# Three 512-token and two 384-token groups in place of six of 384, the first group's first products in halves, attention in pairs of blocks, and weights converted in place

## The chip, the core and the metric

The kernel runs on one core of a Trainium2 chip. The metric is the device time of one execution in microseconds (us). In the traces PE is the matrix engine (PEld its weight loads), DVE the vector engine, ACT the scalar engine, POOL the GpSimd engine, and SP the engine whose queue issues every DMA here.

## What is computed

Three stages follow one another. Attention looks back over a window of 64 positions, the second stage is a two-layer network with a Mish activation, and the third is one with a softmax-weighted activation (SoLU) and a layer norm. All of it is to be exact to fp32.

```python
batch, n_heads, seq, head_dim = (4, 8, 576, 64)          # 2304 tokens, d_model 512
scores = scale * q @ k.T;  mask = (rel >= 0) & (rel < 64)
attn = softmax(where(mask, scores, -1e9));  x = attn @ v  # [2304, 512]
h = x @ w_in                                              # 512 -> 2048
x = (h * tanh(softplus(h))) @ w_out                       # Mish, 2048 -> 512
h = x @ w_in2                                             # 512 -> 1024
solu = h * softmax(h)
out = layernorm(solu) * g_ln @ w_out2                     # 1024 -> 512
```

## The kernel before

**Products.** Each fp32 operand of the network stages is split into a part of 12 bits (hi) and the rest (lo), and a product is three matmuls: hi by hi, hi by lo, lo by hi. The weights come as 64-bit floats: 32 bits in `st[:, :, 1]` (upper) and 32 in `st[:, :, 0]` (lower), side by side, so that each half is read with a stride of two words. A *piece* is 128x512 weights; w_in (called w1) and w_out (w2) have 16 pieces each, w_in2 (w3) and w_out2 (w4) 8 each. One piece costs a load into `st` and six steps: `c_up` (L322) scales the upper half into a tile `wf`, `c_low` (L332) the lower half into `wl`, `c_bits` (L338) and `c_sign` (L344) put the fp32 weight together in `wf`, `c_hi` (L359) rounds it to hi, and `c_lo` (L364) takes lo. `st` and `wf` have 3 buffers each, `wl` has 2. The first 4 pieces lie in a room of their own, `room_b`.

**Attention.** The 2304 tokens are 36 blocks of 64. For one block, `a_qk` writes the scores of 8 heads into one PSUM bank (128x512), and DVE scales and masks them (`a_scale`, L469), takes the maximum (`a_max`, L475) and subtracts it (`a_sub`, L481). ACT takes the exponential (`a_exp`, L489) and DVE the sum (`a_sum`, L493) and its reciprocal (`a_norm`). POOL multiplies (`a_mul`, L504), PE transposes (`a_tr`), ACT copies (`a_pt`), and PE multiplies by the values (`a_pv`). ACT and DVE then write hi and lo of x (`a_x`, `a_xl`). Scores, transposes and results share the pool `ps_a`, two buffers of one bank. The first 6 blocks, which are the first group, go by another way (`a_max0`, L451; `a_exp0`, L459): the mask is added by a matmul, and the exponential takes the maximum as its bias and gives the sum itself, one call for each pair of heads.

**Mish stage.** The tokens are six groups of 384. One *iteration* (j, f) takes group j and 128 hidden units f. `pe_m1` (L574) makes 12 matmuls of 384 columns into `ps_h`, ACT applies Mish (L597), hi and lo of the result are taken (`g_h`, L263 or L267; `g_l`, L283), and `pe_m2` and `pe_m2l` add 8 and 4 matmuls to four accumulators x_0 to x_3 (one bank each). Groups 0 and 1 are done for f 0 to 7 and then for f 8 to 15, so that the weights of the second half are needed later. Their first halves are stored (`part_d`) and added at the end. Attention of group j+1 runs beside the products of group j.

**Third stage.** 18 tiles of 128 tokens: 24 matmuls (L715), the SoLU and the norm on DVE, ACT and POOL, 8 transposes (L763) and 24 matmuls (L788).

**Order.** `Schedule` is a list scheduler that runs while the program is built. Each step has a cost on one or more engines, a due time (from the number of its iteration and tables such as `MISH_AT`, `ATT_AT`, `CONV_PRIO`) and the buffers that it needs, and the scheduler gives out the order of the instructions of each engine. At run time each engine takes its own list strictly in order and waits on semaphores. ACT reloads its function table (ACT_TABLE_LOAD) between an exponential and a Mish.

Of the kernel before, what the change touches and what calls it, by code (L numbers as in the profile page):

```python
# [14 lines left out]
F32 = mybir.dt.float32  # L15
# [9 lines left out]
P = 128  # L25
BLK = 64
LD = 2
CUT = 8
# [6 lines left out]
    "up0": {"act": 0.57, "pool": 0.846}, "up": {"act": 0.57},  # L35
    "pt0": {"act": 0.5}, "x0": {"act": 0.29}, "pt": {"act": 0.5}, "x": {"act": 0.29},
    "w0_hi": {"dve": 0.36, "act": 0.51}, "w0_lo": {"dve": 0.63, "pool": 1.5},
    "w_hi": {"act": 0.51, "dve": 0.36}, "w_lo": {"dve": 0.63, "pool": 1.5},
    "w4_hi": {"act": 0.613}, "w4_lo": {"dve": 0.663},
    "g_hi": {"dve": 0.28, "act": 0.42}, "g_lo": {"dve": 0.48},  # L40
    "x2": {"act": 0.39, "dve": 0.5},
# [15 lines left out]
G_AT = 10.0
K0_LATER = -3.349
W_STEP = 5.115
M4_LATER = -0.753  # L60
# [118 lines left out]
def attention_moe_solu(  # L179
# [27 lines left out]
    GROUPS = [384] * 6  # L207
# [3 lines left out]
    N0 = GROUPS[0] // BLK  # L211
    assert N0 <= NBB
    GMAX = max(GROUPS)
# [35 lines left out]
    st_p = actx.enter_context(tc.tile_pool(name="st", bufs=3))  # L249
# [8 lines left out]
    ps_a = tctx.enter_context(tc.tile_pool(name="ps_a", bufs=2, space=PSUM, side="right"))  # L258
# [62 lines left out]

    def c_up(e, p):  # L322
        p["wf"] = st_p.tile([P, 512], F32, tag="wf", name="wf")
        w = p["st"][:, :, 1].bitcast(F32)
        if e == "act":
            nc.scalar.activation(out=p["wf"], in_=w, func=ACTF.Copy, scale=2.0**-112)  # L326
        else:
            nc.gpsimd.tensor_scalar(
                out=p["wf"], in0=w, scalar1=2.0**-112, scalar2=0.0, op0=ALU.mult, op1=ALU.add
            )  # L330

    def c_low(p):  # L332
# [49 lines left out]
    NI = NF * NG  # L382
    needs += [NI - NF + 4 + W_STEP * (n + 1) for n in range(2 * KD + NF2)]
# [21 lines left out]
    def open_q0():  # L405
        room["q"] = wpool.tile([P, N0 + 1, NP, P], F32, tag="w1", name="room_q")
# [27 lines left out]
    def a_qk(n):  # L434
        ps = ps_a.tile([P, NP, P], F32, tag="a", name="ps_s")
        r = room["r"]
        for p in range(NP):
            early = n < N0
            nc.tensor.matmul(out=ps[:, p, :], lhsT=qt[n][:, p, :], rhs=kt[n][:, p, :], start=True, stop=not early)  # L439
            if early:  # L440

                nc.tensor.matmul(
# [642 lines left out]
```

## Time and profile before

| | |
|---|---|
| time, median of 3 runs | 740.83 us (740.2 to 741.36) |
| the profiled execution's own time | 740.77 us |
| its span, first to last instruction | 739.0 us |
| granted PE clock, mean | 0.988 |
| busy: PE, DVE, ACT, POOL | 706.6, 425.4, 295.8, 156.3 us |

The span leaves 1.77 us of the time outside. Busy time of PE is an upper bound on its work, because neighbouring matmuls overlap in the records: a matmul of 384 columns has a record of 341 ns, and the next one starts after 173 ns. What a stage costs PE is therefore read from how far apart the starts of two stages lie where PE never waits. Busy shares are means over stages with different limits, so the stages are to be read one by one.

### The profile page before, as it was taken

The numbers are of one execution on the slowest core, as the hardware profiler recorded it, in microseconds if no ns is written. First come the engines' busy times: TensorE is split into PE (matmuls) and PEld (weight loads), VectorE is DVE, ScalarE is ACT, GpSimd is POOL, SyncE is SP. The second block draws the span as 40 slices with busy tenths as digits, with TensorE's granted clock in tenths as the row PEclk, the third lists the DMA queues.
The fourth block names the chain that finished last, engine by engine and source line by source line (L and its number), as shares of the span: only waits on it lengthen the run. The fifth ranks groups of instructions, "written<-read, shape, count | busy, mean of one in ns | idle before, by whom it ended". The sixth has DMA issues, their size and how long they took to land.

```text
span 739.0 us, 11115 instructions
## 1 busy us (share of the span) xinstructions
PE 706.6 (96%) x4344; PEld 653.2 (88%) x4344; DVE 425.4 (58%) x734; ACT 295.8 (40%) x551; POOL 156.3 (21%) x176
## 2 busy tenths in 40 slices
PE   6797889699999999999999999999999999999998
PEld 5696789699999999999999999999888888888886
DVE  3999999955645334424434412676575646464642
ACT  4665435454454345334434433345432323232221
POOL 3556644421111011011101110331122111121000
PEclk9899999899999999999999999999999999999999
DMA  8645565652622201302222011331111111111001
GB/s 299 243 155 196 163 213 173 192 178 98 192 83 100 86 30 58 129 29 75 69 88 70 1 44 58 114 114 58 59 43 57 43 43 43 43 44 43 29 16 43
DMA packets 42916, 70.45 MB, mean 95 GB/s; under 512 B 3312, under 2 KB 27376, under 8 KB 42864
## 3 DMA queue, kind: packets, MB, share of 16 engines
q1 hardware_dynamic: 42864, 69.75, 28.6%
q8 instruction: 34, 0.56, 0.3%
q14 instruction: 18, 0.15, 0.1%
HBM read 58.72 MB, written 11.01 MB: 94 GB/s over the span
## 4 chain that ended last, share of the span: by engine, by line
PE 85%; DVE 10%; issue 2%; ACT 1%; DMA 1%; POOL 0%; SPq 0%; DVEq 0%; ACTq 0%; POOLq 0%
PE ps_h L587 24%; PE x L621 16%; PE h L715 14%; PE po L788 13%; PE x L632 8%; PE ps_s L439 4%; DVE wf L346 3%; DVE wf L340 3%; PE pt L763 2%; PE ps_o L541 2%; PE ps_t L518 2%; DVE g L283 1%; DVE w L267 1%; DMA room_q<-qk 0%; DVE su L493 0%
## 5 line engine op out<-in xcount | busy, mean ns | idle before, releaser
L587 PE MATMUL ps_h<-xt,w 128*128 128x384 f32 x1152 | 221.5, 341 | 5.6 <-POOL w L281 2.0
L587 PEld LDWEIGHTS ps_h<-xt,w 128*128 128x128 f32 x1152 | 204.5, 191 | 8.3 <-POOL w L281 2.8
L621 PE MATMUL x<-g,w 128*128 128x384 f32 x768 | 153.5, 340 | 9.4 <-ACT xs L657 6.2
L621 PEld LDWEIGHTS x<-g,w 128*128 128x128 f32 x768 | 134.9, 190 | 12.0 <-ACT xs L657 6.9
L283 DVE SCALAR_TENSOR_TENSOR g<-mc,g 128x384 fp32r<-128x384 f32 x96 | 69.8, 728 | 109.2 <-ACT g L263 108.5
L597 ACT ACTIVATE mc<-ps_h 128x384 f32<-128x384 f32 x96 | 47.0, 490 | 154.9 <-PE ps_h L587 154.6
L715 PE MATMUL h<-w,xs 128*128 128x512 f32 x432 | 104.2, 396 | 0.4 <-DVE y L734 0.4
L788 PE MATMUL po<-w,lz 128*128 128x512 f32 x432 | 102.3, 393 | 0.0
L715 PEld LDWEIGHTS h<-w,xs 128*128 128x128 f32 x432 | 80.8, 188 | 19.6 <-PE x L632 0.7
L504 POOL TENSOR_TENSOR s<-s,rs 128x512 f32<-128x512 f32 x36 | 40.6, 1145 | 257.3 <-DVE rs L498 109.7
L788 PEld LDWEIGHTS po<-w,lz 128*128 128x128 f32 x432 | 80.0, 188 | 16.4
L632 PE MATMUL x<-g,w 128*128 128x384 f32 x384 | 84.1, 340 | 0.0
L632 PEld LDWEIGHTS x<-g,w 128*128 128x128 f32 x384 | 67.6, 189 | 0.7
L334 POOL TENSOR_SCALAR wl<-st 128x512 uint32<-128x512 uint32 x44 | 37.6, 855 | 63.5 <-DMA st<-w_in 20.1
L722 DVE TENSOR_REDUCE nm<-h 128x1 f32<-128x1024 f32 x18 | 22.0, 1224 | 49.1 <-PE h L715 49.1
L263 ACT ACTIVATE g<-mc 128x384 fp32r<-128x384 f32 x87 | 45.8, 526 | 4.9 <-PE x L632 2.2
L326 ACT ACTIVATE wf<-st 128x512 f32<-128x512 f32 x44 | 29.3, 672 | 45.3 <-DMA st<-w_in 21.0
L706 POOL TENSOR_TENSOR xs<-xr,xs 128x512 fp32r<-128x512 f32 x18 | 23.3, 1294 | 95.2 <-ACT xs L701 95.2
L281 POOL TENSOR_TENSOR w<-wf,w 128x512 fp32r<-128x512 f32 x22 | 33.1, 1510 | 43.9 <-DVE w L267 40.3
L346 DVE SCALAR_TENSOR_TENSOR wf<-st,wf 128x512 uint32<-128x512 uint32 x44 | 40.5, 921 | 1.2
L340 DVE SCALAR_TENSOR_TENSOR wf<-wf,wl 128x512 uint32<-128x512 uint32 x48 | 40.8, 851 | 0.1
L701 ACT ACTIVATE xs<-xr 128x512 fp32r<-128x512 f32 x18 | 11.4, 632 | 62.9 <-PE h L715 46.9
(75 smaller groups left out, 671.9 us busy)
## 6 DMA issues: line engine op xcount, KB each, us to landing
qk<-qk SPq DMA_DIRECT2D x30, 512.0 KB, 4.4
st<-w_out SPq DMA_DIRECT2D x24, 512.0 KB, 3.6
st<-w_in SPq DMA_DIRECT2D x20, 512.0 KB, 3.8
v<-v SPq DMA_DIRECT2D x30, 256.0 KB, 2.8
x2d<-xs SPq DMA_DIRECT2D x24, 192.0 KB, 2.1
xr<-x2d SPq DMA_DIRECT2D x18, 256.0 KB, 3.1
out<-o SPq DMA_DIRECT2D x18, 256.0 KB, 2.0
room_b<-w_in SPq DMA_DIRECT2D x4, 512.0 KB, 7.8
```

The costliest lines, as they stand in the source:

```text
L263: nc.scalar.activation(out=hi, in_=x, func=ACTF.Copy, scale=1.0 if g is None else g)
L283: nc.vector.scalar_tensor_tensor(out=lo, in0=x, scalar=1.0 if g is None else g, in1=hi.bitcast(F32), op0=ALU.mult, op1=ALU.subtract)
L334: nc.gpsimd.tensor_scalar(out=p["wl"], in0=p["st"][:, :, 0], scalar1=0.9325 * 2.0**-29, scalar2=0.0, op0=ALU.mult, op1=ALU.add)
L340: nc.vector.scalar_tensor_tensor(out=wb, in0=wb, scalar=3, in1=p["wl"], op0=ALU.logical_shift_left, op1=ALU.bitwise_or)
L346: nc.vector.scalar_tensor_tensor(out=wb, in0=p["st"][:, :, 1], scalar=0x80000000, in1=wb, op0=ALU.bitwise_and, op1=ALU.bitwise_or)
L504: nc.gpsimd.tensor_tensor(out=s, in0=s, in1=rs.to_broadcast([P, NP, P]), op=ALU.mult)
L587: nc.tensor.matmul(out=ps[:, :n], lhsT=w[:, a, k, fs], rhs=x[:, b, k, :n], start=(idx == 0), stop=(idx == len(terms) - 1),)
L597: nc.scalar.activation(out=c[:, :n], in_=ht.pop(i)[:, :n], func=ACTF.Mish)
L621: nc.tensor.matmul(out=acc[j][m][:, :n], lhsT=w[:, a, f % 4, m * P:(m + 1) * P], rhs=g[:, 0, :n], start=(i in opens and a == 0), stop=False,)
L632: nc.tensor.matmul(out=acc[j][m][:, :n], lhsT=w[:, 0, f % 4, m * P:(m + 1) * P], rhs=g[:, 1, :n], start=False, stop=i in closes,)
L715: nc.tensor.matmul(out=h2[t][:, c, :], lhsT=x[:, a, k, :], rhs=wt["w3", c][:, b, k, :], start=(idx == 0), stop=(idx == len(terms) - 1),)
L788: nc.tensor.matmul(out=po[t], lhsT=lz[:, a, f, :], rhs=wt["w4", f // 4][:, b, f % 4, :], start=(c == 0 and idx == 0), stop=(c == 2 and idx ...
```

## The change

- `GROUPS` becomes 512, 512, 512, 384, 384. The first four f of group 0 are done in two halves of 256 columns (`HALF`), so `its` has 84 iterations: 8 of 256 columns, 44 of 512 and 32 of 384 (before: 96 of 384).
- Only the first 4 blocks go the early way (`N0`). All others go in pairs: one instruction works on 128x1024 where two worked on 128x512 (the two copies `a_pt` stay apart). `ps_a` becomes one buffer of two banks for the scores, the transposes and the results of a pair. `a_pt` writes back into the score tile.
- Up to block 15 (`n < N1`) `a_sub` and `a_sum` fall away: `a_exp1` calls the exponential 8 times for a pair with the maximum as bias and the sum as a by-product.
- `a_mul` may go to POOL or to DVE.
- The conversion is done in `st` itself, which has 4 buffers; `wf` and `wl` are gone. `c_low` goes to ACT (POOL for the first two pieces), `c_hi` to ACT and `c_lo` to DVE (the first two pieces' `c_hi` may go to either).
- Due times count PE time (`pos`) in place of iterations, and all tables of numbers are new; of these only the lines below are shown.

```diff
-    "w_hi": {"act": 0.51, "dve": 0.36}, "w_lo": {"dve": 0.63, "pool": 1.5},
+    "w_hi": {"act": 0.54}, "w_lo": {"dve": 0.69},
+    "mul0": {"pool": 1.05, "dve": 0.69}, "mul": {"pool": 2.2, "dve": 1.23},
...
-    GROUPS = [384] * 6
+    GROUPS = [512, 512, 512, 384, 384]
-    N0 = GROUPS[0] // BLK
+    N0 = GROUPS[0] // BLK // 2
+    N1 = (GROUPS[0] + GROUPS[1]) // BLK
-    st_p = actx.enter_context(tc.tile_pool(name="st", bufs=3))
+    st_p = actx.enter_context(tc.tile_pool(name="st", bufs=4))
-    ps_a = tctx.enter_context(tc.tile_pool(name="ps_a", bufs=2, space=PSUM, side="right"))
+    ps_a = tctx.enter_context(tc.tile_pool(name="ps_a", bufs=1, space=PSUM, side="right"))
...
+    def c_low(e, p):
+        w = p["st"][:, :, 0]
+        if e == "act":
+            nc.scalar.activation(out=w, in_=w, func=ACTF.Copy, scale=0.9325 * 2.0**-29)
...
+    def c_bits(p):
+        lw, uw = p["st"][:, :, 0], p["st"][:, :, 1]
+        nc.vector.scalar_tensor_tensor(
+            out=lw, in0=uw, scalar=3, in1=lw, op0=ALU.logical_shift_left, op1=ALU.bitwise_or
         )
...
+    n = GROUPS[0] // 2
+    its = [(0, f, o, o + n) for o in (0, n) for f in range(HALF)]
+    its += [(0, f, 0, 2 * n) for f in range(HALF, CUT)]
+    its += [(1, f, 0, GROUPS[1]) for f in range(CUT)]
+    its += [(j, f, 0, GROUPS[j]) for j in range(2) for f in range(CUT, NF)]
+    its += [(j, f, 0, GROUPS[j]) for j in range(2, NG) for f in range(NF)]
...
+        ns = (n,) if early else (n, n + 1)
+        if early:
+            ps = ps_x2.tile([P, NP, P], F32, tag="x2", name="ps_s")
+        else:
+            ps = ps_a.tile([P, 2 * NP, P], F32, tag="a", name="ps_s")
...
+    def a_exp1(n, ps):
+        s, nm, su = s_t[n]
+        for p in ps:
+            nc.scalar.activation(
+                out=s[:, p], in_=s[:, p], func=ACTF.Exp, bias=nm[:, p:p + 1], accum_out=su[:, p:p + 1]
+            )
...
+            if n < N1:
+                su = step(dict(none=0.0), t + offs[3], a_neg, n, after=[mx], uses=[s, nm])
+                ex = step(dict(act=1.68 + 1.33), t + offs[4], a_exp1, n, range(NP), after=[su], uses=[s])
+                sm = step(dict(act=1.68 + 1.33), t + offs[4], a_exp1, n, range(NP, 2 * NP), after=[ex], uses=[s])
             else:
+                su = step(dict(dve=1.23), t + offs[3], a_sub, n, after=[mx], uses=[s, nm])
+                ex = step(dict(act=1.03 + 2.66), t + offs[4], a_exp, n, after=[su], uses=[s])
+                sm = step(dict(dve=1.2), t + offs[5], a_sum, n, after=[ex], uses=[s])
```

Three places show what the new order makes of it. The first is ACT's list beside the second attention pair of group 1, where L668 is Mish, L520 the exponential of half a pair and L270 the rounding to hi. Before, one pair (L489) with its two table loads, Mish being L597:

```order
L489 ACT_TABLE_LOAD
L489 ACTIVATE s<-s 128x512 x2
L275 ACTIVATE xt<-ps_o 128x4x64 x2
L597 ACT_TABLE_LOAD
L597 ACTIVATE mc<-ps_h 128x384
```

And after the change:

```order
L520 ACT_TABLE_LOAD
L520 ACTIVATE s,su<-s,nm 128x128 x4
L668 ACT_TABLE_LOAD
L668 ACTIVATE mc<-ps_h 128x256
L520 ACT_TABLE_LOAD
L520 ACTIVATE s,su<-s,nm 128x128 x4
L668 ACT_TABLE_LOAD
L668 ACTIVATE mc<-ps_h 128x256
```

The pair that took two table loads takes four here. Up to the last block of group 1 the new list has 11 table loads after the first one, all in front of a half or a whole pair or of the Mish behind it.

The second place is DVE's list where the weights of the second f quarter are converted (`w_737` is w1's, `w_750` w2's; L349 and L355 are `c_bits` and `c_sign`, L290 takes a lo part, L532 scales and masks a pair). Before, the same work (L340, L346) alternates with L267, the rounding to hi, and L283:

```order
L340 SCALAR_TENSOR_TENSOR wf<-wf,wl 128x512
L346 SCALAR_TENSOR_TENSOR wf<-st,wf 128x512
L267 CAST w_516<-wf 128x512
L283 SCALAR_TENSOR_TENSOR g<-mc,g 128x384
L340 SCALAR_TENSOR_TENSOR wf<-wf,wl 128x512
L346 SCALAR_TENSOR_TENSOR wf<-st,wf 128x512
```

And after:

```order
L349 SCALAR_TENSOR_TENSOR st<-st 128x512
L355 SCALAR_TENSOR_TENSOR st<-st 128x512
L636 TENSOR_TENSOR xt<-ps_o,xt 128x4x128
L290 SCALAR_TENSOR_TENSOR w_737<-st,w_737 128x4x128
L532 SCALAR_TENSOR_TENSOR s<-ps_s,mask_n 128x1024
```

The rounding has left DVE, and the lo part, which POOL took for more than half of the w1 and w2 pieces, now stands in DVE's list.

The third place is PE's list around the second and third pair of group 1 (`ps_s` scores, `ps_t` transposes, `ps_o` results, each of them in the one buffer of `ps_a`; `ps_h` is `pe_m1`, and four rows of `pe_m2l` and of `pe_m2` are cut to those printed):

```order
L614 MATMUL ps_o<-s,v 64x64 x16
L658 MATMUL ps_h<-xt,w_737 128x512 x12
L486 MATMUL ps_s<-qk 128x128 x8
L658 MATMUL ps_h<-xt,w_737 128x512 x12
L703 MATMUL x_0_505<-g,w_331 128x256
L703 MATMUL x_1_506<-g,w_331 128x256
L703 MATMUL x_2_507<-g,w_331 128x256
L703 MATMUL x_3_508<-g,w_331 128x256
L579 MATMUL ps_t<-ident,s 128x128 x8
```

Here the scores of one pair stand between the results of the pair two before and the transposes of the pair before it. Before the change, transposes and results of a pair stand together:

```order
L587 MATMUL ps_h<-xt,w_586 128x384 x12
L518 MATMUL ps_t<-ident,s 128x128 x8
L541 MATMUL ps_o<-pt,v 64x64 x16
L621 MATMUL x_0_531<-g,w_926 128x384 x2
L621 MATMUL x_1_532<-g,w_926 128x384 x2
```

## Rows read from the trace of the kernel before

**Rows 1.** Stages: busy us (instructions) of PE, PEld, DVE, ACT, POOL, granted clock, DMA share, GB/s.

```profile
5.15:32.96 27.81, 21.32 (x209) 17.68 (x209) 20.45 (x45) 16.47 (x64) 13.00 (x14) 0.97 0.95 330
32.96:76.24 43.28, 37.08 (x246) 34.39 (x246) 42.35 (x65) 24.90 (x41) 25.01 (x21) 0.90 0.48 161
76.24:150.67 74.43, 63.91 (x363) 60.11 (x364) 71.05 (x97) 33.30 (x62) 35.91 (x34) 0.95 0.60 189
150.67:515.39 364.72, 364.72 (x2498) 360.05 (x2498) 167.85 (x309) 154.63 (x268) 46.05 (x44) 1.00 0.25 82
```

**Rows 2.** Chain of waits, PE in a stretch without waits: start us, us, what.

```profile
196.66 0.87 PE ps_t L518 x8
200.91 1.78 PE ps_s L439 x16
216.08 1.08 PE ps_o L541 x32
206.87 2.08 PE ps_h L587 x12
208.95 1.39 PE x L621 x8
210.34 0.69 PE x L632 x4
...
544.25 5.60 PE h L715 x24
...
537.91 5.47 PE po L788 x24
```

**Rows 3.** PE in order of time: start us, us, engine, line, out<-in, [idle before].

```profile
32.96 8.88 PE L587 MATMUL ps_h<-xt,w 128*128 128x384 f32 x36 [0.94 <-DVE xt L562]
114.45 0.85 PE L632 MATMUL x<-g,w 128*128 128x384 f32 x4
140.50 1.65 PE L621 MATMUL x<-g,w 128*128 128x384 f32 x4 [4.41 <-ACT xs L657]
```

**Rows 4.** DVE, first 160 us: count, duration ns min/median/max, first and last start.

```profile
L346 DVE SCALAR_TENSOR_TENSOR wf<-st,wf x31: 674/693/1673, 37.1 to 151.6; 128x512 uint32<-128x512 uint32 x31
```

**Rows 5.** DVE and POOL in order of time around 56 us.

```profile
56.26 1.64 POOL L281 TENSOR_TENSOR w<-wf,w 128x512 fp32r<-128x512 f32 x1 [0.36 <-DVE w L267]
56.81 1.63 DVE L346 SCALAR_TENSOR_TENSOR wf<-st,wf 128x512 uint32<-128x512 uint32 x1
```

**Rows 6.** Groups by line, whole span: busy us, mean ns of one, idle before.

```profile
L346 DVE SCALAR_TENSOR_TENSOR wf<-st,wf 128x512 uint32<-128x512 uint32 x44 | 40.5, 921 | 1.2
L722 DVE TENSOR_REDUCE nm<-h 128x1 f32<-128x1024 f32 x18 | 22.0, 1224 | 49.1 <-PE h L715 49.1
L442 PE MATMUL ps_s<-room_q 128*128 128x128 bf16 x24 | 6.0, 251 | 0.0
L326 ACT ACTIVATE wf<-st 128x512 f32<-128x512 f32 x44 | 29.3, 672 | 45.3 <-DMA st<-w_in 21.0
L275 ACT ACTIVATE pt<-ps_t 128x512 f32<-128x512 f32 x36 | 20.2, 596 | 9.9 <-PE ps_t L518 9.9
L597 ACT ACTIVATE mc<-ps_h 128x384 f32<-128x384 f32 x96 | 47.0, 490 | 154.9 <-PE ps_h L587 154.6
```

**Rows 7.** DVE and ACT in order of time: first instructions, and a table load.

```profile
7.98 0.69 DVE L451 TENSOR_REDUCE nm<-ps_s 128x4 f32<-128x512 f32 x1 [7.98 <-PE ps_s L442]
...
8.97 0.37 ACT L459 ACTIVATE s<-ps_s,nm 128x128 f32<-128x128 f32 x1 [4.80 <-DVE nm L452]
9.33 0.36 ACT L459 ACTIVATE s<-ps_s,nm 128x128 f32<-128x128 f32 x1
...
171.80 1.28 ACT L489 ACT_TABLE_LOAD   x1
173.09 1.16 ACT L489 ACTIVATE s<-s 128x512 f32<-128x512 f32 x2
```

**Rows 8.** DMA issues: size, median us from issue to landing.

```profile
st<-w_out SPq DMA_DIRECT2D x24, 512.0 KB, 3.6
```

More of the change, by code (lines that the diff above doesn't have):

```diff
@@ L27 @@
 LD = 2
+HALF = 4
 CUT = 8
@@ L434, in a_qk @@
     def a_qk(n):
[L435 to L442, printed above, removed]
-                    out=ps[:, p, :], lhsT=r[:, 0, :P], rhs=r[:, 0, P:] if n == 0 else r[:, 1, :P], start=False, stop=True
-                )
+        early = n < N0
+        ns = (n,) if early else (n, n + 1)
+        if early:
+            ps = ps_x2.tile([P, NP, P], F32, tag="x2", name="ps_s")
+        else:
+            ps = ps_a.tile([P, 2 * NP, P], F32, tag="a", name="ps_s")
+        r = room["r"] if early else None
+        for c, m in enumerate(ns):
+            for p in range(NP):
+                o = ps[:, c * NP + p, :]
+                nc.tensor.matmul(out=o, lhsT=qt[m][:, p, :], rhs=kt[m][:, p, :], start=True, stop=not early)
+                if early:
+                    nc.tensor.matmul(
+                        out=o, lhsT=r[:, 0, :P], rhs=r[:, 0, P:] if n == 0 else r[:, 1, :P], start=False, stop=True
+                    )
         s_t[n] = ps
@@ L580, in pe_m1 @@
         assert ("w1", 0, f) in split_done
-        assert all(b in x_done for b in range(starts[j] // BLK, (starts[j] + GROUPS[j]) // BLK))
+        assert all(b in x_done for b in range((starts[j] + a0) // BLK, (starts[j] + a1) // BLK))
         w = wt["w1", f // 4]
@@ L902, in values @@
+            pv = step(dict(pe=0.648 * len(cps)), t + offs[0], a_pv, n, after=cps, new=[O], uses=[pt, O] + w)
             new = []
@@ L905, in values @@
                 new = [xbuf[j]]
-            x = step(COSTS["x0" if early else "x"], t + offs[9], a_x, n, after=[pv], new=new, uses=[O])
-            xl = step(dict(dve=0.335), t + offs[10], a_xl, n, after=[x], uses=[O])
-            x_of.setdefault(j, []).append(xl)
-            pv_of[n], tr_of[n] = pv, tr
-            if not early:
-                pv.after.append(lv)
-        def attend(ns, t, offs, gate):
-            got = [scores(n, t, offs, gate) for n in ns]
-            if ns[0] < N0:
-                done = [last for last, _, _ in got]
-            else:
-                done = [step(
-                    dict(act=0.55 * len(ns) + 2.8), t + offs[3], a_exp, ns, after=[last for last, _, _ in got],
-                    uses=[s for _, _, (_, s, _, _, _) in got],
-                )] * len(ns)
-            for n, e1, (_, lv, bufs) in zip(ns, done, got):
-                values(n, t, offs, e1, lv, bufs)
+            k = len(cps)
@@ L926, in mish @@
         def mish(i):
-            j, f = its[i]
-            k = GROUPS[j] / 384
+            j, f, a0, a1 = its[i]
+            k = (a1 - a0) / 384
+            pe = pe_of(i)
             h, mc, g = (Buf(x) for x in ("x2" if i in H_X2 else "h", "mc", "g"))
-            o = [i + x for x in MISH_AT]
+            o = [pos[i] + x for x in MISH_AT]
             m1 = step(
-                dict(pe=2.081 * k), o[0], pe_m1, i, after=x_of[j] + [split_of["w1", 0, f]], new=[h],
+                dict(pe=pe / 2), o[0], pe_m1, i, after=list({id(x_of[n]): x_of[n] for n in range((starts[j] + a0) // BLK, (starts[j] + a1) // BLK)}.values()) + [split_of["w1", 0, f]] + ([m1_of[i - 1]] if i else []), new=[h],
@@ L938, in mish @@
+            gl = step(COSTS["g_lo" if a1 - a0 > 256 else "g_lo0"], o[3], g_l, i, after=[gh], uses=[mc, g])
             new = []
```

402 lines of the change are left out of this document (218 added, 184 removed).

## The prediction

> **What bounds the kernel now.** I read the table by stage first, because a share over the whole span mixes stages. From 150.67 to 515.39 PE is busy for all of 364.72 us, DVE for 46% and ACT for 42% [rows 1]: that stage is PE's own and has nothing to give but PE's work. Before 150.67 it is otherwise. In the two stretches from 32.96 to 150.67 DVE is busy 113.4 of 117.7 us, 96%, while ACT has 58.2 and POOL 60.9, and the granted PE clock falls to 0.90 and 0.95, as it does where PE waits. So DVE sets the pace of the first 150 us, and PE that of the rest.
>
> How much PE loses there follows from its undisturbed pitch. Twelve matmuls of 384 columns start 2.08 us apart, and an iteration (2.08 + 1.39 + 0.69) costs 4.16. A pair of blocks costs 1.78 (scores) + 0.87 (transposes) + 1.08 (results) = 3.73, so a block 1.87 [rows 2]. A block of the early way also has four mask matmuls (busy 0.25 us each [rows 6], overlapping); I take 2.3 for it. At 115.14 the twelfth iteration has ended (a row at 114.45 for 4 matmuls, then 0.69 of pitch [rows 2, 3]). By then PE had issued 14 up and 12 down products, 26 x 2.08 = 54.1, and 12 blocks of attention, 6 x 2.3 + 6 x 1.87 = 25.0: work of 79.1 in 115.1 us, a loss of 36.0. To 150.67 come 6 up and 6 down products, 24.9 in 35.5 us, a loss of 10.6, of which one wait for the copy of an accumulator shows 4.4 [rows 3]. The rest of the span has almost none.
>
> Why DVE is full: the four word operations of a piece are 0.68 to 0.69 us when alone, but the sign step's records reach 1.67 [rows 4], with a mean of 0.92 over the span [rows 6]. The order of time shows where: POOL's lo part runs from 56.26 to 57.90, and the sign step beside it, from 56.81, ends at 58.44, as if it had waited for POOL and then taken its 0.69 [rows 5].
>
> **The change part by part.** I follow one point of the program: the first up product of group 1 (PE's iteration 12 in the new order). Before it PE has done iterations 0 to 11 and 16 blocks, two more scores included, all group 1's x must be ready, and behind it come eight iterations on weights that are converted already.
>
> *PE's work.* 512 columns cost 5.47/24 = 0.228 us a matmul at L788 and 5.60/24 = 0.233 at L715 [rows 2]. I take the first, because L788 like the Mish stage accumulates one long chain without a wait. The line through 0.173 at 384 and 0.228 at 512 gives 0.119 at 256, which no row shows; its bounds are 0.116 (by columns) and 0.173 (no gain at all), 0.6 us less and 10 us more over 192 matmuls. The Mish stage is then 44 x 24 x 0.228 + 8 x 24 x 0.119 + 32 x 4.16 = 396.7 against 96 x 4.16 = 399.4, and two blocks lose their mask matmuls (0.9). Together -3.6. So the larger groups alone bring little. By the followed point PE has 8 x 2.85 + 4 x 5.47 (iterations), 4 x 2.3, 7 pairs of scores and 6 of the rest: 44.7 + 9.2 + 12.5 + 11.7 = 78.1.
>
> *DVE up to that point.* Counted in its new list, up to the last lo part of group 1's x: 54 word operations of 512 (bits, sign, lo) at 0.69 [rows 4] = 37.3. Six pairs scaled and reduced, 1024 wide, 1.22 each [rows 6] = 14.6. Seven multiplications that were POOL's, 6.9. Twelve lo parts of Mish, 6.1, and eight roundings, 3.0. The early blocks' maxima, 4.3, ten reciprocals, 3.7, lo parts of x, 5.8 (0.42 for 256, on the line through 0.69 at 512 and 1.22 at 1024), and one copy, 0.7. Sum 82.4. Before, DVE had spent 20.5 + 42.4 + 37 (the same 95% of 76.24 to 115.14) = 100 on the same PE work [rows 1]. What is saved is the subtraction and the sum of 12 blocks, most of the roundings, and the wait for POOL, which has 17 instructions left up to there. The new 0.69 could be wrong in one respect: bits and sign now write with a stride, which no row shows. Bounds: nothing more (reading with that stride costs nothing: 0.693) and 0.92, which would add 8.5. I take 0.69.
>
> *ACT up to that point.* 64 exponentials of 128x128 at 0.36 [rows 7] = 23.0; 34 conversions at 0.67, 15 copies of transposes at 0.60 [rows 6], 15 roundings at 0.63, 10 copies of x and 12 Mish (0.38 to 0.60) = 22.8 + 9.0 + 9.5 + 10.5; table loads 12 x 1.28 = 15.4; the hi parts of Mish and the masks 3.8. Sum 94.0. Neighbours on ACT overlap a little (two exponentials of 512 take 1.16 together [rows 7], and one copy of that size 0.60 [rows 6]); with 0.09 off each large one the lower bound is 85. Before, ACT had less than 16.5 + 24.9 + 33.3 = 74.7 in all of the first 150 us [rows 1]. So ACT goes from half empty to about as full as DVE.
>
> *When the point comes.* DVE starts at 8.0 and ACT at 9.0 [rows 7]. Up to 32.96 DVE stood idle 4.5 of its 25 us, waiting for one block after another. With no full engine I allow 10 for DVE and 6 for ACT, which has more to fill with. DVE: 8 + 82.4 + 10 = 100. ACT: 9 + 89 (middle) + 6 = 104. PE: 78.1 and the 17 that it loses now until the first product at 32.96 [rows 3] (six early blocks and two scores, 15.6, are done by then) = 95. The last decides: 104.
>
> *From there.* Before, 623.9 us follow 115.14. After, the remaining work is less by 3.6 - (79.1 - 78.1) = 2.6. The loss of 10.6 to 150.67 goes, because DVE has some 43 us left to do for the conversion and PE eight iterations of 5.47 and more. ACT, though, has about 50 left for those 55, so I keep 3. Span: 104 + 623.9 - 2.6 - 10.6 + 3 = 717.7, and 1.8 outside it: **719 us**. Own range 711 to 728: the ends of ACT's sum and of the idle times.
>
> *What hides the rest.* In the stage after 150 us a pair waits for scale, maximum, subtraction, two table loads around an exponential of 1024, sum and multiplication, some 9 us by the rows above. PE has 12 us of products between its scores and its transposes in the new list, so I cost it at nothing. If that cover went, 10 pairs would pay the difference.
>
> **The rivals.** *Faster: PE itself is the limit* (702 to 711). ACT at its lower bound (85) and little idle time put it at 97 and DVE at 96, so that they and PE's startup loss meet at 95 to 97, and with nothing lost afterwards the time is 97 + 623.9 - 2.6 - 10.6 + 1.8 = 709 or less. For it: no engine is at 96% any more. Against: three engines that hand work to each other in order, each over 85% full, seldom wait for nothing.
>
> *ACT is the new bound* (728 to 740). Its list has eleven table loads up to the point, because the halves of a pair's exponentials stand apart with a Mish between. ACT's full sum of 94, 12 idle, and then 55 to do beside 55 of PE's work puts the point at 115, with some 8 of waits behind it: 115 + 623.9 - 2.6 - 10.6 + 8 + 1.8 = 735. For it: ACT's in-order list holds the Mish on which PE's down products wait, behind conversions and exponentials. Against: 0.36 and 0.67 are measured with their waits in them.
> The Trainium skill, ScalarE: Activation LUTs, section What ACT_TABLE_LOAD costs, says that a change of tables costs a drain of 1.38 us besides the load's 1.28. By that, eleven loads would add 15 us to ACT, and the estimate worked out from that page would be near 734. The trace does not agree: the load at 171.80 takes 1.28, and the exponential starts at 173.09, at once [rows 7]; so it has no weight of its own here.
>
> *Slower: one score buffer* (742 to 755). Scores, transposes and results of all pairs share one buffer. PE's list has the scores of one pair between the results of another and the transposes of a third, and PE takes its list in order: where the lo part of x, at the end of DVE's list, is late, the scores wait, and all products behind them. It decides from 24 us on: 1.5 us for each of the 16 pairs, or 4 for each of the 6 in the full stretch. For it: in that stretch DVE and ACT are both late. Against: before, PE waited for nothing of the kind after 150 us [rows 1], and the buffer's own chain (1.78 + 1.22 + 0.87 + 1.2 + 1.08 + 1.3 and hops) is some 9 us a pair, against about 13 of PE's work between two pairs' scores in the full stretch.
>
> *Nothing gained* (739 to 742.5): late loads. `st` has four buffers and frees one only after the lo part, where three `st` and three `wf` stood before. In the new list DVE has 5 to 8 us of work between a lo part and the bits step that needs that buffer again, against 3.6 to the landing [rows 8] and 1.3 of ACT. It would take a delay on every second piece.
>
> **How the numbers follow.** Forecast 0.52, faster rival 0.17, ACT 0.17, one buffer 0.10, nothing gained 0.04. All but the last two end under 740: faster by over 0.2% (1.5 us, about what a measurement of this kernel can tell from no change) has 0.86, within it 0.03, slower 0.11. The range for 8 in 10 leaves out the slower rival and the case without gain (0.14), the end of the ACT case (0.04) and the front of the faster one (0.02): 705 to 737.
>
> **What would show it.** Right: iteration 12's first product (L658, 512 columns, all of group 1's x) near 104; DVE's word operations at 0.69 with few long records; DVE and ACT both at 80 to 92% from 33 to 104; POOL almost empty there; PE without waits after about 160. Wrong: PE waits for `ps_s` behind the lo part of x, or `ps_t` waits in the stage after 160 (one buffer); ACT over 95% busy and PE's down products waiting for it (ACT); ACT's and DVE's conversions waiting for DMAs (loads); a 256-column matmul at more than 0.12 us.

## The result and the profile after

The changed kernel takes 720.78 us (median of 4 runs, 719.89 to 721.77) against 740.52 for the kernel before (4 runs on the same chip): ratio 0.9733, 95% interval 0.9714 to 0.9752, 19.7 us faster. The prediction said 719. The profiled execution took 721.44 us, its span 719.6. Its stages, which answer to [rows 1] (the split is at the followed point):

```profile
5.15:32.96 27.81, 22.02 (x200) 19.47 (x199) 21.54 (x43) 18.99 (x73) 6.06 (x6) 0.85 0.87 303
32.96:76.24 43.28, 40.47 (x345) 38.41 (x346) 32.72 (x56) 39.62 (x93) 0.00 (x0) 0.94 0.62 208
76.24:111.21 34.97, 29.80 (x226) 23.88 (x224) 24.53 (x39) 30.87 (x73) 1.90 (x1) 0.90 0.52 172
111.21:150.67 39.46, 39.46 (x207) 32.62 (x206) 30.86 (x45) 32.31 (x54) 0.00 (x0) 1.00 0.64 208
150.67:500.00 349.33, 349.33 (x2058) 313.11 (x2058) 155.05 (x228) 148.26 (x232) 2.59 (x2) 1.00 0.25 85
```

DVE, which was busy 96% from 33 us on, is busy 76% and 70% in the second and third stretch; ACT has gone from half empty to 92% and 88%; POOL has one instruction between 33 and 111 us. The chain that ended last (each piece of work followed back to what released it) shows the same, in shares of the span, before and then after:

```profile
PE 85%; DVE 10%; issue 2%; ACT 1%; DMA 1%; POOL 0%; SPq 0%; DVEq 0%; ACTq 0%; POOLq 0%
PE 90%; ACT 4%; DMA 2%; DVE 2%; issue 1%; SPq 0%; ACTq 0%; DVEq 0%
```

DVE's part of it, some 74 us before, is down to some 14. From 111.21 to 500 PE is busy without a gap, at the upper clock level (1.00, 2.4 GHz), and the profile lists no wait of PE after 111.5 us. What PE still loses lies ahead of that. PE in order of time:

```profile
34.62 6.08 PE L658 MATMUL ps_h<-xt,w 128*128 128x256 f32 x36 [2.02 <-DVE xt L636]
...
56.94 1.70 PE L658 MATMUL ps_h<-xt,w 128*128 128x256 f32 x12 [0.82 <-ACT mc L668]
...
85.50 3.00 PE L658 MATMUL ps_h<-xt,w 128*128 128x512 f32 x12
88.34 1.03 PE L579 MATMUL ps_t<-ident,s 128*128 128x128 f32 x8
94.04 4.08 PE L692 MATMUL x<-g,w 128*128 128x512 f32 x8 [4.66 <-ACT w L270]
98.05 1.79 PE L614 MATMUL ps_o<-s,v 128*64 128x64 f32 x32
...
111.21 8.44 PE L658 MATMUL ps_h<-xt,w 128*128 128x512 f32 x36
...
135.30 2.88 PE L658 MATMUL ps_h<-xt,w 128*128 128x512 f32 x12
138.02 1.98 PE L692 MATMUL x<-g,w 128*128 128x512 f32 x8
139.83 1.07 PE L703 MATMUL x<-g,w 128*128 128x512 f32 x4
140.74 2.88 PE L658 MATMUL ps_h<-xt,w 128*128 128x512 f32 x12
```

The first product comes at 34.62 (32.96 before [rows 3]), and iteration 12's first product, the point that the prediction follows, at 111.21 (predicted 104). Between the two one wait stands out: 4.66 us for the hi part of a w_out piece, a rounding on ACT. From its first matmul to the next row, 94.04 to 98.05, the product behind it takes 4.01 us; after 111 us the same eight matmuls take 1.81 (138.02 to 139.83). PE's clock has fallen; the stretches around it (third column from the end: granted clock) show to which level and how long:

```profile
90.00:92.00 2.00, 0.00 (x0) 0.00 (x0) 1.46 (x3) 1.97 (x3) 0.00 (x0) 1.00 0.00 0
92.00:94.00 2.00, 0.00 (x0) 0.00 (x0) 0.96 (x2) 2.00 (x10) 0.00 (x0) 0.67 0.00 0
94.00:96.00 2.00, 1.96 (x4) 1.33 (x5) 1.95 (x4) 2.00 (x6) 0.00 (x0) 0.50 0.10 23
96.00:98.00 2.00, 2.00 (x5) 1.11 (x4) 1.49 (x5) 1.60 (x7) 0.00 (x0) 0.50 0.72 247
98.00:100.00 2.00, 2.00 (x34) 1.88 (x34) 0.75 (x1) 0.10 (x1) 0.00 (x0) 0.62 0.75 228
```

0.50 is the lower level, 1.2 GHz. Why ACT is late there is read from its list in order of time:

```profile
88.59 1.28 ACT L668 ACT_TABLE_LOAD   x1 [1.66 <-PE ps_h L658]
89.88 0.60 ACT L668 ACTIVATE mc<-ps_h 128x512 f32<-128x512 f32 x1
90.50 1.28 ACT L520 ACT_TABLE_LOAD   x1
91.79 0.40 ACT L520 ACTIVATE s<-s,nm 128x128 f32<-128x128 f32 x1
...
93.34 0.64 ACT L270 ACTIVATE w<-st 128x512 fp32r<-128x512 f32 x1
```

ACT is not late for lack of time: it sat idle for 1.66 us until PE's product (L658) ended at 88.5. Then it takes its list in order: table load, Mish, table load, four exponentials (1.56), and only then the rounding, 0.55. PE waits for ACT, which waited for PE. That sum is 5.3, and PE had 0.87 of transposes of its own meanwhile. Read so, this is a loop through two lists; my first guess, that ACT's sum of work is the bound, is a rival to it.

### The profile page after: what moved, and what is told of

It reads as the page before. It is cut to its first block, busy times and chain, and to the rows that moved or that the text cites. A ratio compares the mean times of both kernels' runs of the same rounds, so it can differ in the third digit from the quotient of the medians.

```text
span 719.6 us, 10174 instructions
## 1 busy us (share of the span) xinstructions
PE 697.3 (97%) x4048; PEld 606.4 (84%) x4048; DVE 385.1 (54%) x626; ACT 334.6 (46%) x633; POOL 48.1 (7%) x75
## 4 chain that ended last, share of the span: by engine, by line
PE 90%; ACT 4%; DMA 2%; DVE 2%; issue 1%; SPq 0%; ACTq 0%; DVEq 0%
PE ps_h L658 26%; PE x L692 18%; PE h L785 14%; PE po L858 14%; PE x L703 9%; PE ps_s L486 4%; PE pt L833 2%; PE ps_o L614 2%; PE ps_t L579 1%; DMA st<-w_in 1%; DMA room_b<-w_in 1%; ACT st L334 1%; ACT st L341 1%; ACT L668 1%; ACT s L520 1%
## 5 line engine op out<-in xcount | busy, mean ns | idle before, releaser
L658 PE MATMUL ps_h<-xt,w 128*128 128x512 f32 (+2 forms) x1008 | 212.8, 361 | 2.8 <-DVE xt L636 2.0
L658 PEld LDWEIGHTS ps_h<-xt,w 128*128 128x128 f32 x1008 | 178.8, 190 | 24.1 <-DVE xt L636 2.2
L692 PE MATMUL x<-g,w 128*128 128x512 f32 (+2 forms) x672 | 149.7, 364 | 4.9 <-ACT w L270 4.7
L692 PEld LDWEIGHTS x<-g,w 128*128 128x128 f32 x672 | 119.0, 190 | 19.6 <-ACT w L270 4.9
L290 DVE SCALAR_TENSOR_TENSOR g<-mc,g 128x512 fp32r<-128x512 f32 (+2 forms) x84 | 51.5, 615 | 137.7 <-ACT g L270 136.7
L668 ACT ACTIVATE mc<-ps_h 128x512 f32<-128x512 f32 (+2 forms) x84 | 44.9, 536 | 134.8 <-PE ps_h L658 133.8
L703 PE MATMUL x<-g,w 128*128 128x512 f32 (+2 forms) x336 | 81.2, 363 | 0.0
L270 ACT ACTIVATE g<-mc 128x512 fp32r<-128x512 f32 (+2 forms) x62 | 36.3, 587 | 22.1 <-PE x L703 20.8
L334 ACT ACTIVATE st<-st 128x512 f32<-128x512 f32 x44 | 29.9, 680 | 9.2 <-DMA st<-w_out 5.7
L486 PEld LDWEIGHTS ps_s<-qk 128*128 128x128 f32 x256 | 31.9, 199 | 1.9 <-DVE xt L636 1.2
L349 DVE SCALAR_TENSOR_TENSOR st<-st 128x512 uint32<-128x512 uint32 x44 | 30.2, 687 | 5.8 <-ACT st L341 5.7
L486 PE MATMUL ps_s<-qk 128*128 128x128 f32 x256 | 32.8, 283 | 0.3 <-DVE xt L636 0.3
```

The lines of the kernel that those rows point to most:

```text
L270: nc.scalar.activation(out=hi, in_=x, func=ACTF.Copy, scale=1.0 if g is None else g)
L290: nc.vector.scalar_tensor_tensor(out=lo, in0=x, scalar=1.0 if g is None else g, in1=hi.bitcast(F32), op0=ALU.mult, op1=ALU.subtract)
L334: nc.scalar.activation(out=w, in_=w, func=ACTF.Copy, scale=2.0**-112)
L349: nc.vector.scalar_tensor_tensor(out=lw, in0=uw, scalar=3, in1=lw, op0=ALU.logical_shift_left, op1=ALU.bitwise_or)
L486: nc.tensor.matmul(out=o, lhsT=qt[m][:, p, :], rhs=kt[m][:, p, :], start=True, stop=not early)
L658: nc.tensor.matmul(out=ps[:, :n], lhsT=w[:, a, k, fs], rhs=x[:, b, k, a0:a1], start=(idx == 0), stop=(idx == len(terms) - 1),)
```

## The experiments

Three theories: **A**, ACT's sum of work sets the pace up to the point; **D**, DVE's does, as before; **P**, PE's own list does, from its first product on, apart from the loop above. Differences below are those of the ratios to the kernel before, times 740.5 us. Each ratio's interval is 1.0 to 1.7 us to either side, so two changed kernels less than some 2 us apart can't be told from one another.

**Taking work away.** Four kernels, in each of which the lists of PE and of the other engines stay as they are.

```diff
         if e == "act":
-            nc.scalar.activation(out=w, in_=w, func=ACTF.Copy, scale=0.9325 * 2.0**-29)
+            pass
...
-            out=lw, in0=uw, scalar=3, in1=lw, op0=ALU.logical_shift_left, op1=ALU.bitwise_or
+            out=lw, in0=uw, scalar=3, in1=lw, op0=ALU.logical_shift_left, op1=ALU.bitwise_and
```


> The changed kernel with every c_low on ScalarE left out (the lower half of a weight then stays unscaled, and c_bits puts it in with an AND instead of an OR, so the weights are other numbers); PE, DVE and every other ACT instruction keep their places in the lists. Up to iteration 12's first product (111.21 us in the changed kernel) that is 17 instructions, 0.57 us apart: 9.7 us less for ACT, nothing less for PE or DVE. If ACT's list sets the pace between 34 and 111 us (my theory, after the trace: ACT is busy 39.6 of 43.3 us there and DVE 32.7), the point comes 6 to 9 us earlier, at 102 to 105, and the time is 711 to 715. If DVE still sets it, or the chain of hand-overs, less than 2 us: 719 to 721.

Measured: 719.77 us, ratio 0.9715 (0.9692 to 0.9738), 1.3 less; point at 108.57.

```diff
-        nc.vector.scalar_tensor_tensor(
-            out=lw, in0=uw, scalar=0x80000000, in1=lw, op0=ALU.bitwise_and, op1=ALU.bitwise_or
-        )
```


> The changed kernel without c_sign (the weights lose their sign); the lists stay otherwise the same. Up to the point that takes 19 instructions of 0.69 us, 13 us, from DVE, a third more than the run without c_low takes from ACT. If ACT sets the pace, the point moves by 0 to 3 us, since DVE only hands each piece to ACT 0.69 us sooner: 717 to 721. If DVE does, 8 to 12 us: 709 to 713.

Measured: 718.56 us, 0.9701 (0.9684 to 0.9717), 2.4 less; first product at 32.92, point at 108.75.

```diff
-        nc.scalar.activation(out=c[:, :n], in_=ht.pop(i)[:, :n], func=ACTF.Mish)
+        nc.scalar.activation(out=c[:, :n], in_=ht.pop(i)[:, :n], func=ACTF.Exp if i < 12 else ACTF.Mish, scale=1e-3 if i < 12 else 1.0)
```


> The changed kernel with an exponential in place of Mish in iterations 0 to 11 (their hidden values are then other numbers): ACT needs no other function table before the point, and ten loads of 1.283 us, 12.8 us, fall away; the lists stay otherwise the same. If ACT's sum of work sets the pace, the point comes 7 to 11 us earlier, at 100 to 104: 709 to 714. If only the one long wait counts (PE waits 4.7 us at 89 us for a hi part that stands in ACT's list behind two table loads, a Mish and four exponentials, and its clock is at the lower level for some 5 us after), 2.6 us of that wait go and perhaps the clock's 3: 714 to 718. If DVE sets the pace, 719 to 721.

Measured: 714.12 us, 0.9643 (0.9623 to 0.9664), 6.7 less; point at 102.75.

```diff
-        if e == "act":
+        if e == "act" and p["name"] not in ("w1", "w2"):
```


> The changed kernel with c_low of all w_in and w_out pieces given to POOL, where it was before the change; the other engines' lists stay the same. ACT loses 9.7 us up to the point, POOL gets 17 x 0.89 = 15 (the price in the trace of before). If ACT sets the pace and DVE has room for the longer records that appear beside POOL's work (DVE is idle 27 us up to the point), the point moves 3 to 8 us forward: 712 to 718. If what the change gained is that POOL no longer runs beside DVE, DVE's word operations go from 0.69 to about 0.9 in the mean and the time does not fall: 719 to 726.

Measured: 721.54 us, 0.9741 (0.9726 to 0.9756), 0.6 more; point at 110.67. DVE's bits and sign steps have records up to 1.14 us again, and the first product comes 1.5 us later (36.10, behind a wait of 4.08 for DVE's lo part of x), so this run is no clean test of ACT's sum.

A fails: 9.7 us less for ACT is worth 1.3 or nothing, and D fails as well, with 13 us less for DVE worth 2.4, most of it ahead of the first product. In both, and with c_low on POOL, the long wait is still there, and still 4.66 (L689 is L692 in the kernel without c_sign):

```profile
91.43 4.08 PE L692 MATMUL x<-g,w 128*128 128x512 f32 x8 [4.66 <-ACT w L270]
91.38 4.08 PE L689 MATMUL x<-g,w 128*128 128x512 f32 x8 [4.66 <-ACT w L270]
94.80 3.90 PE L692 MATMUL x<-g,w 128*128 128x512 f32 x8 [4.66 <-ACT w L270]
```

P has no run of its own, since none takes work from PE: it rests on A and D failing, and on the trace, where PE waits for 6.3 of the 76.6 us from its first product to the point.

Of these four runs only the exponential in place of Mish shortens the wait, because it takes two table loads out of the loop. Its 714.12 lies where the ranges of two theories meet (709 to 714 for ACT's sum, 714 to 718 for the one wait); the row of the wait decides. PE there, in order of time:

```profile
34.17 4.57 PE L658 MATMUL ps_h<-xt,w 128*128 128x256 f32 x36 [2.46 <-DVE xt L636]
87.60 0.50 PE L692 MATMUL x<-g,w 128*128 128x512 f32 x1 [1.98 <-ACT w L270]
88.88 1.89 PE L692 MATMUL x<-g,w 128*128 128x512 f32 x7 [0.78 <-DVE w L290]
102.75 8.43 PE L658 MATMUL ps_h<-xt,w 128*128 128x512 f32 x36
```

4.66 - 1.98 = 2.68, two loads of 1.28 and hardly more. (The Trainium skill, ScalarE: Activation LUTs, section What ACT_TABLE_LOAD costs, gives each change of tables a drain of 1.38 us besides the load; the estimate from that page is that 5.3 should have gone, and this run does not agree.) The clock does not fall here, and from the down product on PE needs 102.75 - 87.60 - 0.78 - 0.31 = 14.1 us to the point; in the changed kernel it is 111.21 - 94.04 - 0.51 = 16.7. So the fallen clock costs 2.6 there. A further part of the 8.5 us at the point is luck: the first 36 matmuls ran at the upper level in this execution (4.57 us) and at the lower one for some of the way in the changed kernel's (6.08). The points of the first two runs have the same 1.5 us of luck in them (4.58 and 4.57).

**Adding work.** What takes nothing away when it goes may still be the next bound.

```diff
-        nc.vector.scalar_tensor_tensor(
-            out=lw, in0=uw, scalar=0x80000000, in1=lw, op0=ALU.bitwise_and, op1=ALU.bitwise_or
-        )
+        for _ in range(2):
+            nc.vector.scalar_tensor_tensor(
+                out=lw, in0=uw, scalar=0x80000000, in1=lw, op0=ALU.bitwise_and, op1=ALU.bitwise_or
+            )
```


> The changed kernel with c_sign done twice (the second one changes nothing), all else in its place: 19 x 0.72 = 13.7 us more for DVE up to the point, where it is idle for 27. Theory that PE itself is the limit from its first product on, apart from the one loop through the lists: the time rises by 1 to 5 us, mostly ahead of the first product, where two of the four or five pieces delay the first hi parts: 721 to 726. Rival (DVE is as near to the limit as before the change): by 10 to 14, 731 to 735.

Measured: 728.06 us, 0.983 (0.9815 to 0.9846), 7.2 more; point at 118.64.

```diff
-        round_12(e, hi, w, p["g"])
+        for _ in range(2):
+            round_12(e, hi, w, p["g"])
```


> The changed kernel with every rounding of a weight to hi done twice, all else in its place: 17 x 0.57 = 9.7 us more for ACT up to the point (two more roundings are DVE's). ACT is idle about 13 us up to there and 2 us in 40 between 36 and 84. If ACT's sum sets the pace or lies just under it, the time rises by 6 to 10: 727 to 731. If PE is the limit with ACT well below, by 0 to 3: 721 to 724. The taking away moved nothing; between the two I expect 4 to 7, since ACT's list has almost no free place: 725 to 728.

Measured: 728.34 us, 0.9834 (0.982 to 0.9848), 7.5 more; point at 117.19.

Of 13.7 us for DVE 7.2 come through, of 9.7 for ACT 7.5. Both doses hit harder than I expected. ACT's 728.34 lies in the range of ACT's sum setting the pace or lying just under it (727 to 731), and the chain that ended last now runs through ACT for 14% of the span, 4% in the changed kernel. (The trace has ACT idle for 3.2 of the 48 us from 36 to 84, not 2 in 40.) DVE's 728.06 lies between the two ranges, P's and the rival's. Of the 7.4 us at its point 3.7 are a later first product (38.36), 1.1 are the clock (the first 36 matmuls take 7.21), and 2.2 are waits for scores behind DVE's lo part of x. Its PE waits up to the point (the transposes, `ps_t`, wait ahead of the first product, for a reciprocal):

```profile
PE x L693 <- ACT w L270: 4.7, 1, 4.7
PE ps_t L580 <- DVE rs L562: 3.7, 1, 3.7
PE ps_h L659 <- DVE xt L637: 3.5, 1, 3.5
PE ps_s L487 <- DVE xt L637: 2.5, 3, 1.6
```

The changed kernel therefore stands on the edge: 2.2 us of ACT's added time found room and 6.5 of DVE's. As far as the trace shows, PE's own list with the loop is the limit, and ACT lies close under it, DVE a little further.

**Back to DVE, and back to POOL.**

```diff
-    N1 = (GROUPS[0] + GROUPS[1]) // BLK
+    N1 = N0
```


> The changed kernel with subtraction and sum on DVE for the six pairs up to block 15 as well (N1 = N0), so one exponential of 1024 for a pair in place of eight with bias and sum. DVE has 12 x 1.22 = 14.6 us more up to the point, ACT about 6 x 2.1 = 12.6 less; the lists are made anew from these costs. If DVE stands as near to the limit as the run with a doubled c_sign says (13.7 us more cost 7.3), the time rises by 4 to 8: 725 to 729. If ACT were the tighter of the two, the time would stay or fall: 716 to 721.

Measured: 725.95 us, 0.9802 (0.9786 to 0.9818), 5.1 more; the point at 115.92. The lists are others here (the loop at 89 us is not in them), so this is the worth of the part as a whole: bias and sum on ACT bring 5 of the 19.7 us, and what they relieve is DVE (busy 30.4 instead of 24.5 us from 76 to 111).

```diff
-        rest(e, lo, w, hi, p["g"])
+        rest("pool" if f % 2 and p["name"] in ("w1", "w2") else e, lo, w, hi, p["g"])
```


> The changed kernel with the lo part of every w_in and w_out piece of odd f on POOL, as more than half of them were before the change; all other instructions keep their places. DVE gets rid of 9 x 0.69 = 6.2 us up to the point, but if POOL's reading holds DVE up, its word operations beside POOL show records of 1.2 to 1.7 us as before [rows 4], and the lo parts that PE waits for take 1.5 instead of 0.69. With DVE not the limit I expect a loss of 0 to 3 us: 720 to 724. If what the change gained were DVE's sum of work alone, the time would fall by 2 to 5.

The run moved more than this says: `f` is there the last value of an outer loop, 7, so all 32 lo parts went to POOL. Measured: 722.56 us, 0.976 (0.974 to 0.978), 2.0 more; point at 111.43. DVE's sign step up to 150 us, in the changed kernel and then in this one (ns, min/median/max):

```profile
L355 DVE SCALAR_TENSOR_TENSOR st<-st x25: 685/694/698, 32.9 to 148.2; 128x512 uint32<-128x512 uint32 x25
```
```profile
L355 DVE SCALAR_TENSOR_TENSOR st<-st x25: 685/694/1694, 33.6 to 149.0; 128x512 uint32<-128x512 uint32 x25
```

The long records of [rows 4] are back as soon as POOL has the lo parts, and gone in the changed kernel. That agrees with the Trainium skill, SBUF — State Buffer, section SBUF: two separate sides: of a DVE operation with two inputs from SBUF and a GpSimd operation that reads SBUF, whichever starts first holds their shared port for its whole length. DVE is still relieved (busy 100.5 instead of 109.7 us from 5 to 151), and that brings no time here: PE waits another 0.68 us for POOL's lo part at the long wait, and the 2.0 us are at the edge of what can be told.

**The size of the first tiles.**

```diff
-HALF = 4
+HALF = 0
```


> The changed kernel without halves (HALF = 0): group 0's products begin with 512 columns, so that all eight of its blocks must be ready before the first one; the lists are made anew. PE then has two more pairs (5.6 us of its work) ahead of its first product, which waits for two more chains of scale, maximum, eight exponentials, multiplication and copies. If the halves are there for the start, the first product comes at 42 to 48 instead of 34.6 and PE's loss at that point grows by 2 to 8 us: 722 to 729. If the start is given back later, because PE is not the limit up to the point: 719 to 721.

Measured: 720.49 us, 0.9733 (0.9715 to 0.9751): no difference. PE's first product and the point:

```profile
46.51 5.44 PE L658 MATMUL ps_h<-xt,w 128*128 128x512 f32 x12 [2.07 <-DVE xt L636]
...
108.93 5.72 PE L658 MATMUL ps_h<-xt,w 128*128 128x512 f32 x24
```

The start is 11.9 us later, and the point 2.3 earlier: PE does attention in the meantime, and from 46.5 on it waits for only 0.7 us in all. In this list there is no loop like that of 89 us. So the halves as such bring nothing here (the lists are made anew); I had expected 2 to 8.

**One part of the change alone**, in the kernel before:

```diff
-        round_12(e, hi, w, p["g"])
+        round_12("act", hi, w, p["g"])
...
-        rest(e, lo, w, hi, p["g"])
+        rest("dve", lo, w, hi, p["g"])
```


> The kernel before, with all roundings of weights on ACT and all lo parts on DVE, each at its old place in the order: of the change, this alone. Up to 115 us DVE loses 21 roundings (13.0 us by the trace of before), takes 14 lo parts (9.7), and no longer runs beside POOL's 20.5 us of lo parts, where its records were up to 1 us longer; POOL keeps c_low and the multiplication. I expect 8 to 12 us less for DVE and 731 to 736. If the change's gain is this alone, 720 to 726. If ACT's later roundings cost as much as they save, 739 to 742.

Measured: 735.51 us, 0.9935 (0.9918 to 0.9952), 4.8 less than the kernel before. Its stages from 32.96 to 115.14 (the second of [rows 1] is 42.35 busy for DVE and 25.01 for POOL):

```profile
32.96:76.24 43.28, 34.56 (x252) 31.36 (x251) 39.78 (x66) 29.45 (x49) 13.60 (x13) 1.00 0.50 163
76.24:115.14 38.90, 35.75 (x229) 34.11 (x228) 33.81 (x52) 24.54 (x47) 13.37 (x15) 1.00 0.60 193
```

Up to 115.14 DVE is busy for 92.9 us instead of 100.9, at the low end of the 8 to 12 less that I expected. PE's granted clock is higher as well, 1.00 instead of 0.95 over that stretch, so the 4.8 us need not be DVE's relief alone. In the old kernel the place of roundings and lo parts is worth about a quarter of the gain.

**Mending the loop.** First an exchange in ACT's list alone (shown are the lists, not the code, with line numbers of the changed kernel; the scheduler's `issue` holds the exponentials of block 14's pair back until the rounding is out):

```diff
-L520 ACT_TABLE_LOAD
-L520 ACTIVATE s,su<-s,nm 128x128 x4
 L270 ACTIVATE w_750<-st 128x512
+L520 ACT_TABLE_LOAD
+L520 ACTIVATE s,su<-s,nm 128x128 x4
```


> The changed kernel with two neighbouring pieces of ACT's list exchanged and nothing else: the rounding to hi of one w_out piece (f 6) in front of the table load and the four exponentials that stand ahead of it. Theory after the first four runs: the wait of 4.66 us, which stayed 4.66 whatever was taken from DVE or ACT, is a loop through the lists (PE's up product, then on ACT table load 1.28, Mish 0.60, table load 1.28, four exponentials 1.56, the rounding 0.55, then PE's down product, with only 0.87 of transposes on PE meanwhile), so the exchange takes 2.84 from it, to about 1.8, and with a wait so short the clock may stay at its upper level behind it, which gives another 2 to 3: time 714.5 to 718.5, 717 if the clock falls nevertheless. Rival (ACT's sum of work decides; the wait only shows where): no work is taken away, so 720 to 722.

Measured: 719.88 us, 0.9719 (0.9701 to 0.9736). PE there:

```profile
89.51 0.49 PE L697 MATMUL x<-g,w 128*128 128x512 f32 x1 [1.71 <-ACT w L275]
92.07 3.35 PE L697 MATMUL x<-g,w 128*128 128x512 f32 x7 [2.06 <-DVE w L295]
```

The wait for ACT falls to 1.71, as worked out, but the lo part of the same piece is late next: on DVE it stood behind three more instructions. So the second kernel moves that one too (DVE's list; a few lines of `issue` hold iteration 10's lo part and the next bits step back until it is out):

```diff
 CAST g<-mc 128x512
-SCALAR_TENSOR_TENSOR g<-mc,g 128x512
+SCALAR_TENSOR_TENSOR w_750<-st,w_750 128x512
 SCALAR_TENSOR_TENSOR st<-st 128x512
+SCALAR_TENSOR_TENSOR g<-mc,g 128x512
 SCALAR_TENSOR_TENSOR st<-st 128x512
-SCALAR_TENSOR_TENSOR w_750<-st,w_750 128x512
```


> The exchange on ACT of the run before (hi part of w_out's piece f 6 in front of the table load and four exponentials), and on DVE the lo part of the same piece directly behind the rounding of iteration 10's Mish; that lo part stood behind three more instructions and took over 2.06 us of the wait when only ACT's list was mended. PE's wait there should fall from 4.66 to 2.0 to 2.4 (Mish of iteration 10 has to come first: 1.71 measured, and 0.4 to 0.6 for the lo part). If the clock stays at its upper level behind so short a wait, as it did behind 1.98 + 0.78 in the run with one table, 4 to 6 us are won against the changed kernel: 715 to 717. If the clock falls all the same: 717.5 to 719. If the wait is only a sign of ACT's sum of work, nothing: 720 to 722.

Measured: 719.68 us, 0.9716 (0.9699 to 0.9733). PE, and the clock:

```profile
89.20 0.49 PE L703 MATMUL x<-g,w 128*128 128x512 f32 x1 [1.70 <-ACT w L281]
89.93 2.70 PE L703 MATMUL x<-g,w 128*128 128x512 f32 x7 [0.23 <-DVE w L301]
93.69 1.98 PE L625 MATMUL ps_o<-s,v 128*64 128x64 f32 x32 [1.07 <-ACT s L293]
...
107.44 8.44 PE L669 MATMUL ps_h<-xt,w 128*128 128x512 f32 x36
```
```profile
90.00:92.00 2.00, 2.00 (x7) 1.58 (x7) 2.00 (x4) 1.99 (x9) 0.00 (x0) 0.68 0.56 86
92.00:94.00 2.00, 0.93 (x8) 0.31 (x8) 1.67 (x3) 2.00 (x8) 0.00 (x0) 0.50 0.43 176
94.00:96.00 2.00, 2.00 (x33) 1.88 (x30) 0.73 (x3) 2.00 (x9) 0.00 (x0) 0.50 0.40 108
96.00:98.00 2.00, 2.00 (x7) 1.53 (x7) 2.00 (x4) 2.00 (x4) 0.00 (x0) 0.61 0.99 322
```

The two waits fall to 1.93, but the copies that now stand behind the rounding are late by 1.07, and the clock falls after all. 4.66 has become 3.00, and the time is 1.3 us below the changed kernel's by the ratios, whose intervals overlap: not a faster version that I could claim. At like mean clocks it is some 2 us (717.7 against 719.9 and 720.1 at 0.993; 719.4 to 720.1 at 0.985 against 721.4 and 721.8 at 0.986 and 0.985), a comparison made only afterwards. My 715 to 717 rested on the clock staying up, and that was wrong.

## Why the prediction was right, and where it was not

**The bound of before, and its end.** Right. The loss of 10.6 us between 115 and 151 is gone entirely, the word operations stand at 0.69 with a longest sign step of 0.70, and writing with a stride of two words costs nothing here (bound 0.92). That DVE's sum of work was what held the kernel is shown in part: DVE leaves the chain that ended last (10% of the span before, 2% now), moving roundings and lo parts in the kernel before gives 4.8, with a higher clock beside it, and giving DVE subtraction and sum back costs 5.1. The doubled sign step's 7.2 says how near DVE still is in the changed kernel, not what held the old one.

**Where the 19.4 us of the span come from**, by the prediction's own account: PE lost 36.0 and 10.6 before and loses 111.2 - 78.1 = 33.1 now, 13.5 less; its work is 3.6 less; and 2.3 more than that is won behind the point (below). Of the 33.1, the prediction's prices put 19.9 ahead of the first product: at 34.62 PE had done four early blocks, two pairs of scores, and one pair's transposes and results, 14.7 us of work. Before, it was 17.4, so the start has become 2.5 worse, and all that is gained is gained behind it. In the changed kernel's profile the chain that ended last reaches the first product through two loads of w_in, one into `room_b` (5.20 us from 14.20) and one into `st` (8.40 us from 19.41). No run takes these loads apart, and without c_sign or without halves the chain does not go through them, so what a quicker start would be worth stays open. By the parts that were tried alone, bias and sum give 5.1, roundings and lo parts off POOL 4.8 in the old kernel, and the halves none; these need not add up.

**The sums of work** held. ACT was put at 89 (85 to 94) and is busy 89.5 up to the point, the sum of the first three stages above. DVE was put at 82.4 and is busy 78.8, which leaves it at 72% from 33 to 104 us, below the 80 to 92% that I named as a sign; ACT is at 89% there. The idle times did not hold: by the same stages ACT idles for 12.7 us up to the point where I allowed 6, and DVE for 24 where I allowed 10. A matmul of 256 columns starts 0.121 us after the last (48 in 5.83; estimate 0.119), a hair over the 0.12 that I called a sign of being wrong, and worth 0.5 us in all; one of 512 starts after 0.227 (12 in 2.72, from 135.30 to 138.02; estimate 0.228).

**The step that failed is "The last decides: 104"**, with ACT as the last. Without c_low ACT's term would be 94, and the time hardly moved. PE with its waits decides, and its term of 95 was too small. To 111.2 it lacks 16.2: the first product is 1.7 later than the 32.96 that I took over from before, with 0.9 less attention done by then; waits after it are 6.3 (4.66 of them the loop); the clock takes 2.6 behind the loop and some 1.5 in the first 36 matmuls; 0.4 is 17.4 rounded to 17. The last 2.8 I can't lay to one row. Up to the point products, scores and results alternate more often than in the stretches from which the pitches were read, and an up product with transposes behind it takes 2.84 (85.50 to 88.34) against 2.72; that this makes up the 2.8 is not shown. The idea that full engines hand work on late was right; putting it into idle time of ACT was not: what counts is which instruction stands behind which, and no sum of busy times shows that.

**Behind the point** it went 5.3 better than I had it (608.4 to the end instead of 613.7): the 3 us that I kept for ACT are not lost, iterations of 5.44 (135.30 to 140.74) instead of 5.47 give 1.2 over 40, and some 1.1 is not sized. So 719 is right to 2 us because +7.2 and -5.3 nearly cancel, and that is luck.

**The rivals.** Faster, PE itself the limit: its mechanism is the nearest to what trace and runs show, its 702 to 711 is not, because it had PE waiting for nothing. ACT the new bound: the sign, ACT over 95% busy, did not come true (92% and 88%), and though PE did wait for a hi part, taking c_low from ACT gave nothing that can be told from noise. One score buffer: PE's wait for scores behind the lo part of x exists and is 0.3 us (2.5 with DVE's added work). Late loads: a piece takes 4.5 us to land instead of 3.6 [rows 8], and no wait of PE ends with one after the first; the part that loads may have in the start is told above.

## What to carry to other kernels

When a change empties the engine that was the bound, look first for the place where two in-order lists wait for each other: such a loop costs its own sum whatever the engines' shares are, and here neither a lighter ACT nor a lighter DVE shortened it. A busy share of 92% is no bound until a dose shows it: taking 10 us away told more about ACT here than its share did, and adding as much showed how little room was left. An order mended at one place shows the next late instruction, so a wait is worth the difference to the second latest, not its length.

## What was not expected of the hardware

PE's granted clock fell to 0.50, the lower level, behind waits of 4.66, of 1.71 and 2.06, and of 1.70 and 0.23, but not behind 1.98 and 0.78 in the run with one table. By windows of 2 us it stayed there for some 7 us in the changed kernel and for 3.4 in the run with c_low on POOL. What decides stays open. Between 18 and 52 us the clock was low as well, for 3 us up to more than 20, in every profile but that of the old kernel with roundings and lo parts moved, and not in the same place from one kernel to the next. The runs of the changed kernel with a mean clock of 0.993 took 719.9 and 720.1 us, those with 0.986 and 0.985 took 721.4 and 721.8.
